# A decay row carried by DMA instead of one-column matmuls, from chunk 10 on, in a gated linear attention and MoE kernel

## The chip, the cores and the metric

The kernel runs on one core of a Trainium2 chip. The metric is the device time of one execution in microseconds (us). A core has five engines with queues of their own: TensorE (PE, with weight loads listed as PEld), VectorE (DVE), ScalarE (ACT), GpSimd (POOL) and SyncE (SP), which here issues every DMA. Each engine executes its queue in order and waits on semaphores for the others.

## The reference

Inputs are q, k, v and alpha in float32, each of 4 batches, 8 heads, 768 steps and 48 channels, and two weight matrices of 384x2048 and 2048x384.

```python
for t in range(S):
    state = alpha[:, :, t, :, None] * state + np.einsum('bhd,bhe->bhde', k[:, :, t], v[:, :, t])
    y[:, :, t] = np.einsum('bhd,bhde->bhe', q[:, :, t], state)
...
x = attn_out.transpose(0, 2, 1, 3).reshape(B * S, H * D)
h = x @ w_in
r = np.maximum(h, 0.0)
return (r * r) @ w_out
```

The output is 3072x384 in float32.

## The kernel before

The 3072 tokens are 24 chunks of 128 steps, six to a batch (NCH). Chunks 0 to 3 are handled two at a time by `add_super`; chunks 4 to 23 by `add_chunk(s)`, with their scores and outputs in `add_scores` and `add_back` (from chunk 8 on two chunks share one `add_scores`). For one chunk the steps are:

- `add_load`: SyncE loads alpha, q, k and v (tiles at, qt, kt, vt), 192 KB each.
- L402 on ACT: L = ln(alpha) into L_s, whose heads are padded from 48 to 64 channels. L407 on POOL: v into bf16.
- `e_p0` on PE: one matmul of 384 columns with an upper triangle sums the logarithms over the steps into a PSUM bank (`pm`); then four matmuls of one column each, with L as weights and a column of ones, put the sums over the whole chunk into four more columns of the same bank, with the channels on the partitions.
- L421 and L425 on ACT: A = exp of the running sums, and Ainv = exp of their negatives, both bf16. L428 and L431 on ACT: the exponentials of the four whole-chunk columns go into `ae_s`, the decay factors of the state, two heads to a column on partitions 0 to 63 and 64 to 127.
- L440 and L443 on DVE: q times A into qA_s, k times Ainv into kI_s. `e_p1q`, `e_p1k` on PE transpose both, L367 copies them (qkT).
- `e_p2` on PE: the scores; L504 on DVE masks them (sm).
- `e_ps` on PE adds k'v to the state in PSUM (st); L538 on DVE (`e_stm`) multiplies the state by `ae_s`; L543 on ACT copies it to bf16 (sb). The last chunk of a batch has none of these three.
- `e_p3a` and `e_p3b` on PE: the chunk's output from the state of the chunk before (sb) and from sm; L365 and a transpose put it into xT_big.

The last running sum of a chunk (row 127 of A) and the sum that the one-column matmuls make are the same quantity, once with the channels along a row and once down the partitions.

The feed-forward part follows group by group: `add_moe1` (x by w_in on PE, relu on ACT in L790, square on DVE in L798) and `add_moe2` (gT by w_out, copy to ob in L828 or L830, store in L837).

All instructions are written out in one order, which a planner (`Plan`) makes in Python: each step has an engine, a planned duration, dependences and a latency, and a list scheduler gives it a start; `plan.order` is sorted by these starts, and the steps are emitted in that order, so each engine's queue is fixed by it. "DMA" is the planner's engine for loads and "OUT" for stores, both emitted on SyncE; a store is placed 3.5 us (OUT_LATE) after its data. `gate` lets `e_p0` of a chunk start only a certain lead ahead of the feed-forward progress. Ahead of the plan, seven matmuls of 512 columns on a zero tile (`warm`) run on PE, and before the first `add_moe2` step idle stretches of the plan on PE are filled with matmuls of 256 columns (`DUMMY`).

Of the kernel before, what the change touches and what calls it, by code (L numbers as in the profile page):

```python
# [8 lines left out]
FP32 = mybir.dt.float32  # L9
BF16 = mybir.dt.bfloat16  # L10
AF = mybir.ActivationFunctionType
# [45 lines left out]
def after(op, x=0.0):  # L57
    return (op, x)
# [86 lines left out]
def kernel(  # L145
# [10 lines left out]
    nc = tc.nc  # L156
    B, H, S, D = q.shape
    HD = H * D
    P = 128
    DP = 64  # L160
    NP = H // 2
# [17 lines left out]
    consts = ctx.enter_context(tc.tile_pool(name="consts", bufs=1))  # L179
    big = ctx.enter_context(tc.tile_pool(name="big", bufs=1))  # L180
    LB = 6
    loads = ctx.enter_context(tc.tile_pool(name="loads", bufs=LB // 2))
    work = ctx.enter_context(tc.tile_pool(name="work", bufs=4))
# [6 lines left out]
    banks = [ctx.enter_context(tc.tile_pool(name=f"bank{i}", bufs=1, space=PSUM)) for i in range(5)]  # L190
# [1 line left out]
    nc.scalar.preload_act_table_set("natural_log_exp_and_others")  # L192

    HF = P // 2
    warm = consts.tile([P, 512], BF16)
    nc.vector.memset(warm, 0.0)
    ones_f = consts.tile([P, P], FP32)
    nc.gpsimd.memset(ones_f, 1.0)
# [2 lines left out]
        out=utri_f, in_=ones_f, compare_op=ALU.is_ge, fill=0.0,  # L201
# [4 lines left out]
        out=sutri_f, in_=ones_f, compare_op=ALU.is_ge, fill=0.0,  # L206
# [10 lines left out]
    for src, dst in ((utri_f, half_in), (sutri_f, half_ex)):  # L217
        nc.vector.memset(dst, 0.0)
        for ab in range(2):
            h = slice(ab * HF, ab * HF + HF)  # L220
            nc.vector.tensor_copy(dst[h, h], src[h, h])
    for ab in range(2):
        h = slice(ab * HF, ab * HF + HF)
# [8 lines left out]
    w_out_b = consts.tile([P, FT, d_model], BF16)  # L232

    NBUF = 4
    L_s = big.tile([P, NBUF, H, DP], BF16)
    nc.gpsimd.memset(L_s[:, :, :, D:], 0.0)
    qA_s = big.tile([P, NBUF, H, DP], BF16)
    nc.gpsimd.memset(qA_s[:, :, :, D:], 0.0)
    ident_bf = consts.tile([P, P], BF16)
    make_identity(nc, ident_bf)  # L240
    kI_s = big.tile([P, NBUF, H, DP], BF16)
    nc.gpsimd.memset(kI_s[:, :, :, D:], 0.0)
    ae_s = big.tile([P, NBUF, NP, 2], FP32)
    nc.vector.memset(ae_s, 0.0)
    xT_big = big.tile([P, KT, n_tok], BF16)

    def pin(ins):
        tc.keep_in_program_order(ins)

    def mm(*a, **kw):  # L250
        pin(nc.tensor.matmul(*a, **kw))  # L251

    def tr(*a):
        pin(nc.tensor.transpose(*a))  # L254
# [6 lines left out]
    GLA_BANKS = sl_bank[0:2]  # L261
# [4 lines left out]
    def psum(op, shape, dt):  # L266
        i = op.slot.bank
        return banks[i].tile(shape, dt, name=f"bank{i}")
# [6 lines left out]
    def add(eng, dur, emit, *deps, **kw):  # L275
        return plan.add(Op(eng, dur, emit, deps, **kw))
# [115 lines left out]
    def add_chunk(s):  # L392
        d = C[s]
        b, c = divmod(s, NCH)
        i = s % NBUF
        L, qA, kI, ae = L_s[:, i], qA_s[:, i], kI_s[:, i], ae_s[:, i]
        old = C[s - NBUF].get("end") if s >= NBUF else None
        g = dict(prio=-10.0 + s * 0.01)
        last = c == NCH - 1

        def e_ln():
            pin(nc.scalar.activation(L[:, :, 0:D], d["at"], AF.Ln))  # L402
        ln = d["use_at"] = add("ACT", 0.41, e_ln, d["ld_at"], old, prio=-15.0 if s < EARLY else -5.0)

        def e_vb():
            d["vb"] = work.tile([P, H, D], BF16, name="vb", bufs=4)
            pin(nc.gpsimd.tensor_copy(d["vb"], d["vt"]))  # L407
        vb = d["use_vt"] = add("POOL", 0.55, e_vb, d["ld_vt"], old, prio=-5.0)

        def e_p0():  # L410
            pm = d["pm"] = psum(p0, [P, 512], FP32)
            mm(pm[:, 0:HD], lhsT=utri_b[:, 0, :], rhs=L[:, :, 0:D], start=True, stop=True)
            for p in range(NP):
                mm(pm[:, HD + p:HD + p + 1], lhsT=L[:, 2 * p:2 * p + 2, :], rhs=ones_col,
                   start=True, stop=True)
        p0 = Op("PE", 0.27, e_p0, [ln], takes=GLA_BANKS, lat=0.17, **g)
        p0.gla = s

        def e_A():
            d["A"] = work.tile([P, H, D], BF16, name="A")  # L420
            pin(nc.scalar.activation(d["A"], d["pm"][:, 0:HD].rearrange("p (h d) -> p h d", h=H), AF.Exp))  # L421

        def e_Ai():
            d["Ai"] = work.tile([P, H, D], BF16, name="Ainv")
            pin(nc.scalar.activation(d["Ai"], d["pm"][:, 0:HD].rearrange("p (h d) -> p h d", h=H), AF.Exp, scale=-1.0))  # L425

        def e_ae0():
            pin(nc.scalar.activation(ae[0:64, :, 0], d["pm"][0:64, HD:HD + NP], AF.Exp))  # L428

        def e_ae1():  # L430
            pin(nc.scalar.activation(ae[64:128, :, 1], d["pm"][64:128, HD:HD + NP], AF.Exp))  # L431
        plan.add(p0)
        a_ = add("ACT", 0.38, e_A, p0, **g)
        ai = add("ACT", 0.38, e_Ai, p0, after(a_), **g)
        ae0 = add("ACT", 0.18, e_ae0, p0, after(ai), **g)
        ae1 = add("ACT", 0.19, e_ae1, p0, after(ae0), **g)
        p0.gives = ae1

        def e_qA():
            pin(nc.vector.tensor_mul(qA[:, :, 0:D], d["qt"], d["A"]))  # L440

        def e_kI():
            pin(nc.vector.tensor_mul(kI[:, :, 0:D], d["kt"], d["Ai"]))  # L443
        mq = d["use_qt"] = add("DVE", 0.47, e_qA, a_, d["ld_qt"], old, **g)
        mk = d["use_kt"] = add("DVE", 0.47, e_kI, ai, d["ld_kt"], old, **g)

        def e_p1q():
            d["pT"] = psum(p1q, [P, 2 * NP, P], BF16)
            for p in range(NP):
                tr(d["pT"][:, p, :], qA[:, 2 * p:2 * p + 2, :], ident_bf)  # L450

        def e_p1k():
            for p in range(NP):
                tr(d["pT"][:, NP + p, :], kI[:, 2 * p:2 * p + 2, :], ident_bf)
        p1q = plan.add(Op("PE", 0.22, e_p1q, [mq], takes=GLA_BANKS, **g))
        p1k = plan.add(Op("PE", 0.22, e_p1k, [mk, after(p1q)], lat=0.15, **g))

        def e_cp(lo, hi):
            if lo == 0:
                d["qkT"] = work.tile([P, 2 * NP, P], BF16, name="qkT")  # L460
            cast(cpk if lo else cp, d["qkT"][:, lo:hi, :], d["pT"][:, lo:hi, :])
        if s < EARLY:
            cp = add({"ACT": 0.49, "DVE": 0.34}, 0, lambda: e_cp(0, NP), p1q, **g)
            cpk = add({"DVE": 0.34, "ACT": 0.49}, 0, lambda: e_cp(NP, 2 * NP), p1k, after(cp, -9.0), **g)
        else:
            cp = cpk = add("DVE", 0.61, lambda: e_cp(0, 2 * NP), p1k, **g)
        p1q.gives = cpk

        d.update(cps=[cp, cpk], mk=mk, vb_op=vb, ae1=ae1, kI=kI, ae=ae)
        if s < PAIRS:  # L470
            add_scores(s, 1)
            add_back(s)
        elif s % 2:
            add_scores(s - 1, 2)
            add_back(s - 1)
            add_back(s)
# [90 lines left out]
    def add_super(u):  # L567

        d = SUP[u]
        i = 2 * u % NBUF  # L570
        pair = (C[2 * u], C[2 * u + 1])
        L, qA, kI, ae = L_s[:, i:i + 2], qA_s[:, i:i + 2], kI_s[:, i:i + 2], ae_s[:, i:i + 2]
        old = [C[2 * u - NBUF + ab].get("end") for ab in range(2)] if u >= 2 else []
        g = dict(prio=-10.0 + u * 0.02)
        any_ = (0, 1)
# [4 lines left out]
        ln = d["use_at"] = add("ACT", 0.73, e_ln, d["ld_at"], *old, prio=-15.0)  # L580
# [20 lines left out]
        p0 = [Op("PE", 0.53 if t else 0.33, lambda t=t: e_p0(t), [ln], takes=SUP_BANKS, lat=0.17, **g) for t in any_]  # L601
# [10 lines left out]
        a_, ai = [None, None], [None, None]  # L612
# [5 lines left out]
        def e_ae(j):  # L618
            h = slice(HF * j, HF * j + HF)
            tot = d["pm"][1][h, HD:HD + 2 * NP].rearrange("p (n a) -> p a n", a=2)  # L620
            pin(nc.scalar.activation(ae[h, :, :, j], tot, AF.Exp))
        ae0 = add("ACT", 0.19, lambda: e_ae(0), p0[1], after(ai[1]), **g)
        ae1 = add("ACT", 0.19, lambda: e_ae(1), p0[1], after(ae0), **g)
# [79 lines left out]
        for ab in any_:  # L703
            s = 2 * u + ab
# [40 lines left out]
            if s:  # L745
                p3a = c["p3a"] = plan.add(Op("PE", 0.2, e_p3a, [cq, before], takes=SUP_BANKS, **g))
            p3b = c["p3b"] = plan.add(Op("PE", 0.5, e_p3b, [*sm, *vb, after(p3a)], takes=None if s else SUP_BANKS,
                                         lat=0.15, **g))
# [12 lines left out]
    RELU_PRIO = -20.0  # L761
    RELU_PRIO0 = 0.0
    DUMMY = 1
    sq = {}
    prog = {"m1": 0.0, "m2": 0.0}

# [124 lines left out]
    plan.run(gate)  # L891


    wp = banks[4].tile([P, 512], FP32, name="bank4")
    for _ in range(7):
        mm(wp, lhsT=warm[:, 0:P], rhs=warm, start=True, stop=True)
    pe_end = None
    for op in plan.order:
        if op.eng == "PE":
            if getattr(op, "moe", (0,))[0] == 2:  # L900
                pe_end = None
                DUMMY = 0
            if pe_end is not None and DUMMY:
                n = max(0, int((op.start - pe_end - 0.2) / 0.11))
                if n:
                    wp = banks[4].tile([P, 512], FP32, name="bank4")
                for _ in range(n):
                    mm(wp[:, 0:256], lhsT=warm[:, 0:P], rhs=warm[:, 0:256], start=True, stop=True)
            pe_end = op.start + op.dur
        op.emit()  # L910
# [28 lines left out]
```

## Time and profile before

| | |
|---|---|
| median of 3 runs | 188.93 us (188.61 to 189.2) |
| the profiled execution | 187.66 us, of which the span from the first to the last instruction is 185.9 |
| granted TensorE clock, mean | 0.999 |
| PE busy | 178.4 us |
| DVE busy | 133.8 us |
| ACT busy | 122.6 us |
| DMA queue 1 | 99152 packets, 29.89 MB, 68.1% of 16 engines' span |

The profile is one execution; the median is of others. All times in the text that are points of time count from the span's start. Matmuls are pipelined, so the length shown for one reaches into the next, and starts tell more than lengths. In the lists of groups a line gives the operation, the tiles, the shape, the count, the busy time, the mean of one in ns and the idle time before it with what ended it. L251 and L254 are the lines of the helpers for matmuls and transposes, L367 and L365 those of the copy helper.

### The profile page before, as it was taken

How to read it: one execution, taken by the hardware profiler on the slowest of the kernel's cores; microseconds unless marked ns; L12 is line 12 of the kernel's file. 1: busy time of each engine (PE TensorE's matmuls, PEld its weight loads, DVE VectorE, ACT ScalarE, POOL GpSimd, SP SyncE). 2: the span in 40 equal slices, each digit the busy share in tenths (PEclk: the TensorE clock that was granted, in tenths of full speed). 3: DMA queues.
4: the chain of work that ended last, by engine and by line, in shares of the span. 5: the costliest groups of instructions: out<-in, count | busy, mean ns of one | idle time of the engine just before them, and what ended most of it. 6: DMA issues, size and time to landing. Idle time of an engine off the chain costs nothing.

```text
span 185.9 us, 5105 instructions
## 1 busy us (share of the span) xinstructions
PE 178.4 (96%) x2037; PEld 134.1 (72%) x2037; DVE 133.8 (72%) x280; ACT 122.6 (66%) x282; POOL 29.6 (16%) x47
## 2 busy tenths in 40 slices
PE   6889899999999999999999999999999999999992
PEld 2666684667887878878878878777868778767761
DVE  7688679875999986876976966866987976842400
ACT  3577779455896896776676776667778668434621
POOL 5044777411012111111020020020020000000000
PEclk9999999999999999999999999999999999999999
DMA  5999999899899999999997984691011011011112
GB/s 146 261 280 339 385 370 331 175 223 205 161 206 209 236 199 231 184 231 201 189 222 162 216 166 101 157 212 61 0 42 46 2 48 42 4 42 42 46 43 84
DMA packets 99176, 30.22 MB, mean 163 GB/s; under 512 B 92112, under 2 KB 98000, under 8 KB 99152
## 3 DMA queue, kind: packets, MB, share of 16 engines
q1 hardware_dynamic: 99152, 29.89, 68.1%
q8 instruction: 16, 0.26, 0.5%
q14 instruction: 8, 0.07, 0.1%
HBM read 25.17 MB, written 4.72 MB: 161 GB/s over the span
## 4 chain that ended last, share of the span: by engine, by line
PE 88%; DMA 3%; ACT 3%; SPq 2%; DVE 1%; issue 0%
PE bank L251 77%; PE bank L254 7%; DMA at<-in_alpha_dram 3%; PE sc L251 2%; PE st L251 2%; SPq L360 2%; DVE qkT L367 1%; ACT raw L691 1%; ACT L_s L579 0%; DVE qA_s L627 0%; ACT w_in_b L304 0%; DVE st L721 0%; ACT r L790 0%; ACT ob L830 0%; ACT A L610 0%
## 5 line engine op out<-in xcount | busy, mean ns | idle before, releaser
L251 PE MATMUL bank<-xT_big,w_in_b 128*128 128x256 bf16 (+2 forms) x600 | 73.1, 269 | 0.0
L251 PE MATMUL bank<-w_out_b,gT 128*128 128x384 bf16 x384 | 72.4, 326 | 0.0
L790 ACT ACTIVATE r<-bank 128x512 bf16<-128x512 f32 x96 | 56.9, 602 | 18.8 <-PE bank L251 16.5
L251 PEld LDWEIGHTS <-w_in_b 128*128 128x128 bf16 x600 | 52.5, 98 | 9.2
L798 DVE TENSOR_TENSOR gT<-r 128x512 bf16<-128x512 bf16 x96 | 45.2, 493 | 17.1 <-ACT r L790 16.6
L251 PEld LDWEIGHTS <-gT 128*128 128x128 bf16 x384 | 35.1, 97 | 17.8
L407 POOL CAST vb<-vt 128x384 bf16<-128x384 f32 x20 | 10.9, 550 | 92.7 <-PE bank L251 45.6
L367 DVE COPY qkT<-bank 128x1024 bf16<-128x1024 bf16 (+1 forms) x26 | 16.5, 649 | 6.3 <-PE bank L254 6.2
L830 ACT COPY ob<-bank 128x384 f32<-128x384 f32 x20 | 9.6, 479 | 14.6 <-PE bank L251 14.6
L504 DVE TENSOR_TENSOR sm<-sc,utri_b 128x512 bf16<-128x512 f32 x24 | 15.4, 684 | 2.0 <-PE sc L251 2.0
L365 ACT CAST xn<-bank 128x384 bf16<-128x384 f32 x24 | 10.9, 481 | 5.8 <-PE bank L251 5.7
L440 DVE TENSOR_TENSOR qA_s<-qt,A 128x384 bf16<-128x384 f32 x20 | 11.5, 577 | 3.8 <-ACT A L421 3.7
L251 PEld LDWEIGHTS <-qkT 64*128 64x128 bf16 (+2 forms) x304 | 10.4, 98 | 4.9 <-issue 2.5
L421 ACT ACTIVATE A<-bank 128x384 bf16<-128x384 f32 x20 | 9.9, 494 | 6.2 <-PE bank L251 6.2
L367 DVE COPY xT_big<-bank 128x384 bf16<-128x384 bf16 x21 | 7.4, 354 | 8.3 <-PE bank L254 8.2
L443 DVE TENSOR_TENSOR kI_s<-kt,Ainv 128x384 bf16<-128x384 f32 x20 | 11.3, 567 | 0.0
L543 ACT CAST sb<-st 128x384 bf16<-128x384 f32 x16 | 7.6, 476 | 5.2 <-DVE st L538 5.2
L402 ACT ACTIVATE L_s<-at 128x384 bf16<-128x384 f32 x20 | 10.0, 520 | 0.5 <-DMA at<-in_alpha_dram 0.4
L504 DVE TENSOR_TENSOR sm<-bank,utri_b 128x512 bf16<-128x512 f32 x16 | 10.2, 681 | 0.0
L251 PE MATMUL bank<-warm 128*128 128x256 bf16 (+1 forms) x41 | 8.2, 333 | 2.0 <-DVE both L216 1.3
L425 ACT ACTIVATE Ainv<-bank 128x384 bf16<-128x384 f32 x20 | 9.9, 496 | 0.0
L251 PE MATMUL bank<-vb,sm 128*128 128x48 bf16 (+1 forms) x224 | 9.6, 183 | 0.0
(70 smaller groups left out, 176.3 us busy)
## 6 DMA issues: line engine op xcount, KB each, us to landing
at<-in_alpha_dram SPq DMA_DIRECT2D x20, 192.0 KB, 3.9
qt<-in_q_dram SPq DMA_DIRECT2D x20, 192.0 KB, 3.7
kt<-in_k_dram SPq DMA_DIRECT2D x20, 192.0 KB, 4.0
vt<-in_v_dram SPq DMA_DIRECT2D x20, 192.0 KB, 3.7
out_dram<-ob SPq DMA_DIRECT2D x20, 192.0 KB, 2.3
wo<-in_moe_w_out_dram SPq DMA_DIRECT2D x4, 768.0 KB, 6.8
wi<-in_moe_w_in_dram SPq DMA_DIRECT2D x3, 768.0 KB, 8.0
at<-in_alpha_dram SPq DMA_DIRECT2D x2, 384.0 KB, 4.9
```

The source lines that it names most:

```text
L251: pin(nc.tensor.matmul(*a, **kw))
L254: pin(nc.tensor.transpose(*a))
L365: pin(nc.scalar.copy(out_t, in_t))
L367: pin(nc.vector.tensor_copy(out_t, in_t))
L402: pin(nc.scalar.activation(L[:, :, 0:D], d["at"], AF.Ln))
L407: pin(nc.gpsimd.tensor_copy(d["vb"], d["vt"]))
L421: pin(nc.scalar.activation(d["A"], d["pm"][:, 0:HD].rearrange("p (h d) -> p h d", h=H), AF.Exp))
L440: pin(nc.vector.tensor_mul(qA[:, :, 0:D], d["qt"], d["A"]))
L443: pin(nc.vector.tensor_mul(kI[:, :, 0:D], d["kt"], d["Ai"]))
L504: pin(nc.vector.tensor_mul(d["sm"][:, hh], d["sc"][hh], utri_b.to_broadcast([P, NP, P])))
L790: pin(nc.scalar.activation(box["r"][:, 0:w], box["ph"][:, 0:w], AF.Relu))
L798: pin(nc.vector.tensor_mul(gT[g][:, f0:f0 + per, lo * P:lo * P + n], r, r))
```

## The change

From chunk 10 on (`TURN = 10`) the four one-column matmuls and the two exponentials L428 and L431 are left out. A is written in float32 into a tile `Af` of the order (half j, channel d, pair n), so that consecutive channels of a head lie four floats apart, and L440 reads it in that order. Two DMAs on SyncE (planner's engine "SPD", planned at 0.4 us and a latency of 4.0 us) carry row 127 of `Af` into `ae_s`, 48 partitions of four floats each; `ae_s` has its last two axes exchanged for this. The planner is given 0.17 instead of 0.27 us for `e_p0`, and the bank is given back after Ainv. In the start, the warm tile is 128 columns wide and read four times over, nine matmuls of 512 and two of 128 columns take the place of seven of 512, and idle stretches before 8.0 us of the plan get half as many dummies.

```diff
-    warm = consts.tile([P, 512], BF16)
+    warm = consts.tile([P, P], BF16)
...
+    TURN = 10
+    AE_LAT = 4.0
...
-    ae_s = big.tile([P, NBUF, NP, 2], FP32)
+    ae_s = big.tile([P, NBUF, 2, NP], FP32)
...
-        L, qA, kI, ae = L_s[:, i], qA_s[:, i], kI_s[:, i], ae_s[:, i]
+        L, qA, kI, ae = L_s[:, i], qA_s[:, i], kI_s[:, i], ae_s[:, i].rearrange("p j n -> p n j")
...
-            for p in range(NP):
+            for p in range(NP if s < TURN else 0):
                 mm(pm[:, HD + p:HD + p + 1], lhsT=L[:, 2 * p:2 * p + 2, :], rhs=ones_col,
                    start=True, stop=True)
-        p0 = Op("PE", 0.27, e_p0, [ln], takes=GLA_BANKS, lat=0.17, **g)
+        p0 = Op("PE", 0.27 if s < TURN else 0.17, e_p0, [ln], takes=GLA_BANKS, lat=0.17, **g)
...
+        def split(x, s):
+            if s < TURN:
+                return x.rearrange("p (h d) -> p h d", h=H)
+            return x.rearrange("p (n j d) -> p n j d", n=NP, j=2)
+
         def e_A():
-            d["A"] = work.tile([P, H, D], BF16, name="A")
-            pin(nc.scalar.activation(d["A"], d["pm"][:, 0:HD].rearrange("p (h d) -> p h d", h=H), AF.Exp))
+            if s < TURN:
+                d["A"] = work.tile([P, H, D], BF16, name="A")
+            else:
+                d["Af"] = work.tile([P, 2, D, NP], FP32, name="Af", bufs=2)
+                d["A"] = d["Af"].rearrange("p j d n -> p n j d")
+            pin(nc.scalar.activation(d["A"], split(d["pm"][:, 0:HD], s), AF.Exp))
...
-        ae0 = add("ACT", 0.18, e_ae0, p0, after(ai), **g)
-        ae1 = add("ACT", 0.19, e_ae1, p0, after(ae0), **g)
-        p0.gives = ae1
+
+        def e_aed():
+            for j in range(2):
+                pin(nc.sync.dma_start(out=ae_s[HF * j:HF * j + D, i, j], in_=d["Af"][P - 1:P, j]))
+        if s < TURN:
+            ae0 = add("ACT", 0.18, e_ae0, p0, after(ai), **g)
+            p0.gives = ae1 = add("ACT", 0.19, e_ae1, p0, after(ae0), **g)
+        else:
+            p0.gives = ai
+            ae1 = add("SPD", 0.4, e_aed, a_, lat=AE_LAT, **g)
 
         def e_qA():
-            pin(nc.vector.tensor_mul(qA[:, :, 0:D], d["qt"], d["A"]))
+            if s < TURN:
+                pin(nc.vector.tensor_mul(qA[:, :, 0:D], d["qt"], d["A"]))
+            else:
+                v4 = "p (n j) d -> p n j d"
+                pin(nc.vector.tensor_mul(qA[:, :, 0:D].rearrange(v4, j=2), d["qt"].rearrange(v4, j=2), d["A"]))
...
+    COLD = 8.0
...
-    wp = banks[4].tile([P, 512], FP32, name="bank4")
-    for _ in range(7):
-        mm(wp, lhsT=warm[:, 0:P], rhs=warm, start=True, stop=True)
+    def idle_mm(n, w):
+        wp = banks[4].tile([P, 512], FP32, name="bank4")
+        for _ in range(n):
+            mm(wp[:, 0:w * P], lhsT=warm, rhs=warm[:, None, :].to_broadcast([P, w, P]), start=True, stop=True)
+
+    idle_mm(9, 4)
+    idle_mm(2, 1)
...
-                n = max(0, int((op.start - pe_end - 0.2) / 0.11))
+                n = max(0, int((op.start - pe_end - 0.2) / (0.22 if pe_end < COLD else 0.11)))
                 if n:
-                    wp = banks[4].tile([P, 512], FP32, name="bank4")
-                for _ in range(n):
-                    mm(wp[:, 0:256], lhsT=warm[:, 0:P], rhs=warm[:, 0:256], start=True, stop=True)
+                    idle_mm(n, 2)
```

## The prediction

> **What bounds the kernel now.** I read the page's busy times and its chain first.
>
> ```profile
> PE 178.4 (96%) x2037; PEld 134.1 (72%) x2037; DVE 133.8 (72%) x280; ACT 122.6 (66%) x282; POOL 29.6 (16%) x47
> ...
> PE 88%; DMA 3%; ACT 3%; SPq 2%; DVE 1%; issue 0%
> ```
>
> PE is busy 96% of the span and carries 88% of the chain that ended last. A busy PE need not be a full one, so I looked next at the table of stretches, and at the starts of consecutive matmuls in the timeline.
>
> ```profile
> 60.00:100.00 40.00, 39.99 (x461) 31.40 (x460) 32.04 (x67) 29.16 (x70) 4.84 (x9) 1.00 0.98 205
> 100.00:140.00 40.00, 40.00 (x455) 31.16 (x454) 30.56 (x65) 28.89 (x69) 3.13 (x6) 1.00 0.56 124
> 140.00:183.00 43.00, 42.49 (x419) 31.75 (x416) 23.13 (x50) 23.79 (x53) 0.00 (x0) 1.00 0.11 38
> ```
>
> The columns are the stretch, its length, busy time of PE, PEld, DVE, ACT and POOL, granted clock, DMA share and GB/s. PE has 0.5 us idle in 123 us, at full clock. Here lie chunks 10 to 23 (chunk 10's L421 starts at 68.2, chunk 23's at 157.2). So in the part that the change rewrites, time taken off PE's queue comes off the end, and a late input to PE is paid in full. DVE is 80% busy up to 100, ACT 73%. The DMA share is 0.98 until 100 and 0.11 at the end.
>
> Then chunk 14 in the timeline (start, length, engine, line):
>
> ```profile
> 95.86 0.33 PE L251 MATMUL bank<-L_s,utri_b 128*128 128x384 bf16 x1
> ...
> 96.03 0.24 PE L251 MATMUL bank<-ones_col,L_s 128*128 128x1 bf16 x4
> ...
> 96.13 0.81 PE L251 MATMUL bank<-w_out_b,gT 128*128 128x384 bf16 x4
> ...
> 96.30 0.49 ACT L421 ACTIVATE A<-bank 128x384 bf16<-128x384 f32 x1 [0.57 <-PE bank L251]
> ...
> 96.83 0.56 DVE L440 TENSOR_TENSOR qA_s<-qt,A 128x384 bf16<-128x384 f32 x1 [0.40 <-ACT A L421]
> ...
> 98.08 0.37 PEld L254 LDWEIGHTS <-qA_s 128*128 128x128 bf16 x4
> ...
> 99.50 0.56 DVE L538 TENSOR_TENSOR st<-st,ae_s 128x384 f32<-128x384 f32 x1
> ```
>
> Starts tell what a matmul costs the queue, since its length overlaps the next: the four one-column matmuls hold PE from 96.03 to 96.13, 0.10 us, not the 0.24 shown. qA is ready at 97.39 and PE takes it at 98.08, so it has 0.69 us to spare. In chunk 13 it is less: qA starts at 88.29, ends at 88.85, and its weights load at 89.12.
>
> ```profile
> 88.29 0.56 DVE L440 TENSOR_TENSOR qA_s<-qt,A 128x384 bf16<-128x384 f32 x1
> ...
> 89.12 0.37 PEld L254 LDWEIGHTS <-qA_s 128*128 128x128 bf16 x4
> ```
>
> Last, SyncE and the DMAs:
>
> ```profile
> 80.56 0.59 SPq L837 DMA_DIRECT2D out_dram<-ob  x1
> ```
> ```profile
> at<-in_alpha_dram SPq DMA_DIRECT2D x20, 192.0 KB, 3.9
> out_dram<-ob SPq DMA_DIRECT2D x20, 192.0 KB, 2.3
> ```
>
> The ob of that store ends at 80.54 (L830, 80.06 + 0.48): SyncE stood waiting for it although the plan places each store 3.5 us after its ob. So SyncE runs about 3 us ahead of its own order while loads fill the queue. A load lands 3.9 us after issue; the late stores, on an idle DMA, 1.8 (the least of the 20).
>
> **The change part by part.**
>
> *One-column matmuls.* Fourteen chunks lose four each. The cost is 0.10 us (96.03 to 96.13, likewise 82.23 to 82.33), in chunk 13 0.13 (87.19 to 87.32). 14 x 0.10 to 14 x 0.13 is 1.4 to 1.8 us; I take 1.5, as the short gap is the commoner. It is all on PE's full stretch. A may also start some 0.08 us sooner, since the matrix product ends at 96.19 and the last one-column result at 96.27.
>
> *L428 and L431.* Twenty-eight ACTIVATEs at 0.17 us go, 4.8 us of ACT. ACT has 27% idle, and PE does not wait for it in these stretches: 0. The bank is given back sooner, also 0.
>
> *A in float32, d in steps of four floats.* ACT writes and DVE (L440) reads 384 elements, each 16 bytes from the last. The type costs nothing by the rows: L365 writes 128x384 bf16 in 481 ns, L830 the same size in f32 in 479; L538 reads f32 in 557, L440 bf16 in 577. No row has such a step. The bounds: nothing, or one more element time per element, by the slopes between sizes: ACT (L579 with 768 elements, L402 with 384) (844 - 520)/384 = 0.84 ns, so +0.32 us; DVE (L504 with 512, L538 with 384) (684 - 557)/128 = 0.99 ns, so +0.38 us. A gain is excluded, as nothing is read less often. I take 0, because neither engine's rows here change with the bytes of an element; both ends stay in the range. The Trainium skill, page "Advanced Engine Details and Errata", section "SBUF Cachelines", speaks against the change: an SBUF line has 16 bytes, and accesses that go to another line each time pay a penalty, which this step makes all of them. No run here shows it; by that page the forecast would move towards the first rival.
>
> *The two DMAs.* Each writes 48 pieces of 16 bytes. Queue 1's 68.1% of 16 x 185.9 us over 99152 packets is 20 ns a packet, so 96 more, plus completions, are about 0.12 us of DMA per chunk: nothing, beside 3.9 us a load. SyncE pays two issues of 0.33 to 0.9 us (the stores' least; the loads' usual when the queue is full), and both wait for A. SyncE being 3 us early, it will stand there, and behind it stand the next loads, at, qt, kt and vt of chunks 12 to 23, and stores. Who waits for them: L402 and L407 of later chunks. L402 of chunk 12 follows its load's landing by 1.2 us (69.2, 70.4), of chunk 15 by 2.8 (81.3, 84.1), of chunk 14 by 6.0, of chunk 16 by 10.5. Only the first few are near; cost 0 to 1 us once, and I take 0.1. A gain is excluded, as nothing before the wait goes sooner.
>
> *The multiplication of the state, L538.* It now waits for a DMA. In chunk 14 it starts 2.7 us after A's end (96.79). The diff plans 0.4 + 4.0 us between A and the matmuls of st, so it will stand about 5 us after A. From A's end the DMAs take 2 x 0.35 us of issue and 1.8 (idle) to 3.9 us (loaded): 2.5 to 4.6, inside the plan, since SyncE is early and the loads in front drain meanwhile. What is late next is sb: 100.57 becomes about 103, and its readers are st of chunk 15 at 104.17 and the pair's sb matmuls at 108.27. Cover is left, and PE has MoE work to order in between: 0. Without that cover each us is a us.
>
> *Start.* All that is before chunk 10 keeps its order. The smaller warm tile makes a shorter memset (0.27 us now), nine matmuls of 512 columns and two of 128 fill what was idle before the first L_s matmul at 5.42, and fewer dummies follow. The seven of now run from 1.25, 3.17 us with a last one of 0.63, so they start 0.42 us apart; nine from 1.1 end near 5.0, and two small ones by 5.3: before 5.42, 0.1 us late at worst. The matmul at 5.42 already runs at full pace (the next starts at 5.58, 384 columns in 0.16), so there is no slow clock to cure. And the chain of this part is not PE's: it is the second alpha load (4.32 to 10.52), then L579. I take 0, with -0.1 to +0.1.
>
> Sum on the profiled execution: span 185.9 - 1.5 + 0.1 = 184.5; its time 187.66 (1.76 outside the span) becomes 186.3. The median lies 1.27 above that run, at 188.93, and becomes 187.5.
>
> **The rivals.**
>
> *The step of 16 bytes hurts on both engines* (17%). qA comes 0.32 + 0.38 - 0.08 = 0.62 us later. Spare is 0.27 in chunks like 13; in chunks like 14 the tightest is kI (97.85, taken at 98.41), 0.56. Seven odd chunks lose 0.35, seven even 0.06: +2.9 - 1.5 = +1.4, 190.3. For: L440 and L421 gain a pattern that no row has. Against: equal times for 2 and 4 byte elements. It decides from 0.49 us of lateness on, where seven times 0.22 eat the gain; DVE alone (0.30 late) costs only 0.2, giving 187.6.
>
> *The factors land late and DVE stands at L538* (15%). With loads in front unfinished, 0.7 + 4.9 us (the slowest store landing) is 5.6 against 5.0. Six such chunks (10, 12 to 16) lie in the full DMA stretch. DVE is in order, so qA, sm and gT stand behind it; after about 0.3 us of spare (chunk 13) the remaining 0.3 x 6 = 1.8 us reach PE: 189.2. Against: the wait for A drains the queue.
>
> *Loads held behind the waits starve L402* (8%). Chunks 12, 13 and 15 lose up to 1 us of ACT each, of which I put half on PE: 188.9.
>
> *The change doesn't shorten the queue* (5%): the new order leaves PE a gap of 0.1 us where the matmuls were, and the time stays 188.9. Against: 0.5 us idle in 123.
>
> **How the numbers follow.** The forecast, 187.5, has 55%. Its own range is 186.8 (1.8 saved, 0.1 at the start, no load wait, and 0.2 of PE's idle time) to 188.1 (the load wait at 1 us less a little). For 8 in 10 the range reaches up to the step's rival, and down to all the bounds together: 186.7 to 190.3. 0.3%, 0.57 us, is about what a measurement of this kernel can tell from no change. Faster needs under 188.36: the forecast's 55% and some 7% of milder rivals, 62%. Within 0.3%: half of the two rivals near 188.9 and the last, 14%. Slower: the step's rival and worse forms of the others, 24%.
>
> **What would show it.** Right: PE from 60 to 183 still without idle, the L_s matmul followed at once by the next, A and L440 at 0.49 and 0.56 us after chunk 10 as before it, L538 about 5 us after A with no DMA among what DVE waits for, SyncE waiting at the new DMAs for A. Wrong: L440 near 0.94 us or L421 near 0.8 with PE waiting for qA; DVE waiting for a DMA at L538; ACT waiting for alpha loads at L402.

## The result and the profile after

The change made the kernel about 1% slower: 190.47 us median (189.96 to 191.9, 8 runs) against 188.92 of the kernel before in the same comparison, a ratio of 1.0103 (95% interval 1.0073 to 1.0134). The profiled execution took 191.44 us with a span of 189.7, so it is one of the longer ones. The lines of the code have moved: L421, L440, L443, L538, L402 and the matmul and transpose helpers are now L432, L462, L465, L560, L404, L253 and L256.

The stretches first (PE, PEld, DVE, ACT, POOL, clock, DMA share, GB/s):

```profile
60.00:100.00 40.00, 38.77 (x420) 28.93 (x419) 31.43 (x62) 28.58 (x59) 6.30 (x8) 1.00 0.88 183
100.00:140.00 40.00, 39.38 (x422) 29.58 (x421) 31.85 (x63) 28.20 (x56) 3.01 (x6) 1.00 0.68 145
140.00:183.00 43.00, 42.86 (x422) 31.78 (x420) 26.43 (x56) 26.29 (x51) 0.80 (x1) 1.00 0.11 37
```

PE, which had 0.5 us idle in these 123 us, now has 2.0. More of its waiting stands at the weight loads of the transposes, which need qA and kI. The list of waits has it (total, times, longest):

```profile
PEld L256 <- DVE kI_s L465: 2.9, 11, 0.5
PEld L256 <- DVE qA_s L462: 2.8, 9, 0.6
```

In the kernel before the list had one such wait for qA of L440, and none for kI of L443:

```profile
PEld L254 <- DVE qA_s L440: 0.3, 1, 0.3
```

The groups by form (busy us, mean ns, idle before) show why qA and kI are late:

```profile
L462 DVE TENSOR_TENSOR qA_s<-qt,Af 128x384 bf16<-128x384 f32 x14 | 12.3, 881 | 6.1 <-ACT Af L432 5.4 <-DMA qt<-in_q_dram 0.7
...
L432 ACT ACTIVATE Af<-bank 128x384 f32<-128x384 f32 x14 | 12.1, 866 | 2.6 <-PE bank L253 2.3
```

The same two operations in the kernel before:

```profile
L440 DVE TENSOR_TENSOR qA_s<-qt,A 128x384 bf16<-128x384 f32 x20 | 11.5, 577 | 3.8 <-ACT A L421 3.7
...
L421 ACT ACTIVATE A<-bank 128x384 bf16<-128x384 f32 x20 | 9.9, 494 | 6.2 <-PE bank L251 6.2
```

Chunk 14 in the timeline, to be held against the same chunk before:

```profile
99.31 0.33 PE L253 MATMUL bank<-L_s,utri_b 128*128 128x384 bf16 x1
...
99.67 0.87 ACT L432 ACTIVATE Af<-bank 128x384 f32<-128x384 f32 x1
...
100.58 1.12 DVE L462 TENSOR_TENSOR qA_s<-qt,Af 128x384 bf16<-128x384 f32 x1 [0.25 <-ACT Af L432]
...
101.61 0.55 DVE L465 TENSOR_TENSOR kI_s<-kt,Ainv 128x384 bf16<-128x384 f32 x1
101.71 1.17 SPq L449 DMA_DIRECT2D ae_s<-Af  x2
101.74 0.23 PEld L256 LDWEIGHTS <-qA_s 128*128 128x128 bf16 x4 [0.60 <-DVE qA_s L462]
...
102.21 0.23 PEld L256 LDWEIGHTS <-kI_s 128*128 128x128 bf16 x4 [0.24 <-DVE kI_s L465]
```

Before, qA lay ready 0.69 us ahead of its weight load; now the load stands 0.60 us and starts 0.04 us after qA's end, then stands again for kI. This is the longest of the waits and not a usual one: the q times A of this chunk takes 1.12 us, that of the other thirteen 0.85 to 0.89, and why it is longer stays open. The one-column matmuls are gone: the next matmul starts at 99.47, 0.16 after the L_s matmul.

### The profile page after: what moved, and what is told of

It is laid out like the page before. It is cut to its first block, busy times and chain, and to the rows that moved or that the text cites. A ratio compares the mean times of both kernels' runs of the same rounds, so it can differ in the third digit from the quotient of the medians.

```text
span 189.7 us, 5000 instructions
## 1 busy us (share of the span) xinstructions
PE 181.0 (95%) x1978; PEld 131.7 (69%) x1979; DVE 138.4 (73%) x278; ACT 124.9 (66%) x256; POOL 32.0 (17%) x47
## 4 chain that ended last, share of the span: by engine, by line
PE 74%; ACT 9%; DMA 6%; DVE 5%; issue 2%; SPq 2%; ACTq 0%
PE bank L253 63%; PE bank L256 7%; DMA at<-in_alpha_dram 6%; ACT r L813 2%; ACT Af L432 2%; PE sc L253 2%; SPq L362 2%; PE st L253 2%; DVE kI_s L465 1%; DVE qA_s L462 1%; ACT Ainv L436 1%; DVE gT L821 1%; DVE qkT L369 1%; ACT raw L713 1%; ACT A L432 1%
## 5 line engine op out<-in xcount | busy, mean ns | idle before, releaser
L253 PE MATMUL bank<-xT_big,w_in_b 128*128 128x256 bf16 (+2 forms) x599 | 73.4, 268 | 0.1
L253 PE MATMUL bank<-w_out_b,gT 128*128 128x384 bf16 x384 | 72.7, 326 | 0.0
L253 PEld LDWEIGHTS <-w_in_b 128*128 128x128 bf16 x600 | 53.0, 98 | 10.5 <-issue 1.2
L821 DVE TENSOR_TENSOR gT<-r 128x512 bf16<-128x512 bf16 x96 | 46.2, 507 | 16.3 <-ACT r L813 15.7
L253 PEld LDWEIGHTS <-gT 128*128 128x128 bf16 x384 | 35.4, 98 | 17.8
L409 POOL CAST vb<-vt 128x384 bf16<-128x384 f32 x20 | 13.5, 676 | 93.2 <-DMA vt<-in_v_dram 46.5
L853 ACT COPY ob<-bank 128x384 f32<-128x384 f32 x22 | 10.6, 480 | 13.5 <-PE bank L253 13.5
L462 DVE TENSOR_TENSOR qA_s<-qt,Af 128x384 bf16<-128x384 f32 x14 | 12.3, 881 | 6.1 <-ACT Af L432 5.4
L253 PEld LDWEIGHTS <-qkT 64*128 64x128 bf16 (+2 forms) x304 | 10.5, 97 | 5.6 <-issue 2.7
L432 ACT ACTIVATE Af<-bank 128x384 f32<-128x384 f32 x14 | 12.1, 866 | 2.6 <-PE bank L253 2.3
L465 DVE TENSOR_TENSOR kI_s<-kt,Ainv 128x384 bf16<-128x384 f32 x20 | 12.7, 633 | 0.0
L404 ACT ACTIVATE L_s<-at 128x384 bf16<-128x384 f32 x20 | 10.4, 526 | 2.2 <-DMA at<-in_alpha_dram 2.1
L256 PE MATMUL bank<-ident_bf,qA_s 128*128 128x128 bf16 x96 | 9.4, 220 | 1.3 <-DVE qA_s L462 0.6
L253 PE MATMUL bank<-warm 128*128 128x256 bf16 (+2 forms) x39 | 8.7, 355 | 1.9 <-DVE both L216 1.1
```

What stands on the lines that cost most here:

```text
L432: pin(nc.scalar.activation(d["A"], split(d["pm"][:, 0:HD], s), AF.Exp))
L462: pin(nc.vector.tensor_mul(qA[:, :, 0:D].rearrange(v4, j=2), d["qt"].rearrange(v4, j=2), d["A"]))
L821: pin(nc.vector.tensor_mul(gT[g][:, f0:f0 + per, lo * P:lo * P + n], r, r))
```

## The experiments

The theory was the first rival of the prediction: the step of 16 bytes makes A and q times A late, and PE pays. Against it stood two others: SyncE's waits for A hold loads and factors back, or the planner's new order is worse by itself. Each ratio is against the kernel before in the same comparison, whose median was 188.1 to 188.7 us; several expectations in us were set from 188.9, and so lie a little high.

**The step alone.** `step_only`, on the kernel before:

```diff
-            d["A"] = work.tile([P, H, D], BF16, name="A")
...
+            if s < TURN:
+                d["A"] = work.tile([P, H, D], BF16, name="A")
...
+            else:
+                d["Af"] = work.tile([P, 2, D, NP], FP32, name="Af", bufs=2)
+                d["A"] = d["Af"].rearrange("p j d n -> p n j d")
...
```

> The kernel before, with A alone changed from chunk 10 on: float32, written by ACT and read by DVE with 16 bytes from element to element; the one-column matmuls, their exponentials and the plan's durations stay, no DMA is added. Theory (the step of 16 bytes makes A and q times A late for PE): A 0.86 us and q times A 0.86 us instead of 0.49 and 0.56, PE waits for qA, and the time is before plus about 3 us (the 1.55 us that the change lost plus the 1.5 us of PE that it saved): 191.9, 190.9 to 193. Rival (SyncE's waits for A hold the loads back): as before, 188.9 within 0.3. Rival (the new order): as before.

Measured: 193.03 us, ratio 1.0251 (1.0207 to 1.0294), 4.7 us slower, just past the end of the expected range, 193. A takes 872 ns and q times A 860. There is no new DMA in it, and it loses more than the whole change does, as nothing is saved in it. Its waits:

```profile
PEld L255 <- DVE qA_s L450: 3.6, 10, 0.6
PEld L255 <- DVE kI_s L453: 2.0, 9, 0.3
```

**The DMAs without the step.** `dma_no_step`, on the changed kernel:

```diff
-                d["A"] = d["Af"].rearrange("p j d n -> p n j d")
+                d["A"] = d["Af"].rearrange("p j d n -> p (j d n)").rearrange("p (n j d) -> p n j d", n=NP, j=2)
```

> The changed kernel with A in float32 but in one unbroken row per step, so that ACT and DVE write and read neighbours; the two DMAs move the same number of pieces of 16 bytes at the same place in the order, but the four floats of a piece are then neighbouring channels, so the decay factors from chunk 10 on are wrong ones. Theory (step): A and q times A back to 0.49 and 0.56 us, the 1.5 us of PE come off: 187.5, 187.0 to 188.2. Rival (waits on SyncE and at the state's multiplication): still near the changed kernel, 190 to 190.5, with ACT waiting for alpha loads. Rival (order): also near 190.

Measured: 186.23 us, ratio 0.9892 (0.9861 to 0.9923), with the two operations back:

```profile
L462 DVE TENSOR_TENSOR qA_s<-qt,Af 128x384 bf16<-128x384 f32 x14 | 7.8, 556 | 2.2 <-ACT Af L432 2.2
L432 ACT ACTIVATE Af<-bank 128x384 f32<-128x384 f32 x14 | 6.9, 491 | 2.6 <-PE bank L253 2.3
```

The new DMAs and SyncE's waits for A, and the planner's new order, are all in this kernel, so they are not what made the change slow. Both rivals fall with it. Between this kernel and the changed one lies the step alone: 1.0103 / 0.9892 = 1.0213, or 4.0 us. The time is below the expected 187.0 to 188.2: the change of the start, which the expectation took at nothing, is worth 0.5 us (below), and the kernel before stood at 188.29 here.

Both kernels execute the same 1978 matmuls. PE is busy 178.1 us of a span of 184.8 here and 181.0 of 189.7 in the changed kernel. So of the 4.9 us between these two executions 2.9 lie inside what the profile lists as busy and only 2.0 in idle time. A stretch that shows no idle time is thus no proof that PE waits for nothing.

**The saving alone.** `no_factors` leaves out L428, L431 and the one-column matmuls from chunk 10 on, and puts nothing in their place (`p0` planned at 0.17).

> The kernel before without the one-column matmuls and the two exponentials from chunk 10 on, and with nothing in their place: the state is multiplied by factors of an earlier chunk. It shows what leaving them out is worth by itself. Theory (step) and rival (waits): 14 times 0.10 to 0.13 us of PE, 187.4, 187.0 to 187.7. Rival (the new order that 0.17 for 0.27 us brings costs by itself): 188.9 or more.

Measured: 186.64 us, ratio 0.9930 (0.9902 to 0.9958): 1.3 us by the ratio, 1.65 by the medians. The saving is about the expected one, 1.4 to 1.8 us; the time in us is below the expected range, which was set from 188.9. The rival that the new order costs by itself falls.

**The start alone.** `start_only` is the kernel before with the warm tile, `idle_mm` and `COLD` of the change.

> The kernel before with the start alone changed: the narrow warm tile, nine and two matmuls ahead, half as many dummies before 8 us of the plan. All theories: 188.9 within 0.3, since the chain of the start runs over the second alpha load.

Measured: 187.72 us, ratio 0.9975 (0.9954 to 0.9996). The median hides the kind of the gain: the executions lie between 187.48 and 187.96, those of the kernel before in the same comparison between 187.51 and 189.43. The long ones are gone. The expectation, no change within 0.3 us, missed this. I come back to it below.

**How wide a step costs.** Three layouts on the changed kernel: A and factors in bfloat16 (`bf16_step8`: both tiles declared BF16), float32 with two heads interleaved (`step8`) or eight (`step32`). The line of `step8`, whose other lines bring the sums, q and qA into the same order of heads, and then that of `step32`:

```diff
...
-                d["A"] = d["Af"].rearrange("p j d n -> p n j d")
+                d["A"] = d["Af"].rearrange("p j d n -> p (j d n)").rearrange("p (x d m) -> p m x d", x=4, m=2)
...
```
```diff
-                d["A"] = d["Af"].rearrange("p j d n -> p n j d")
+                d["A"] = d["Af"].rearrange("p j d n -> p (j d n)").rearrange("p (d n j) -> p n j d", n=NP, j=2)
```

> The changed kernel with A and the decay factors in bfloat16 in the same order: the step from element to element is 8 bytes instead of 16, the DMAs move pieces of 8 bytes, all is computed. Theory (two elements must share 16 bytes): A 0.49 and q times A 0.56 us, time as with the unbroken rows, 186.3, 185.8 to 187.0, and so faster than both kernels. Rival (any step other than one element costs): A and q times A between 0.6 and 0.9, 188 to 190.5.

> The changed kernel with A in float32 with a step of 8 bytes (two heads interleaved instead of four). The DMAs move as many pieces of 16 bytes as before, but the floats of a piece are not those of one channel, so the decay factors from chunk 10 on are wrong ones. Theory (two elements must share 16 bytes): 0.49 and 0.56 us, 186.3, 185.8 to 187.0. Rival (the cost grows with the step): about a third of the extra, A 0.6 and q times A 0.66 us, 187 to 188.

> The changed kernel with A in float32 with a step of 32 bytes (all eight heads interleaved); again the factors from chunk 10 on are wrong ones. Theory (each element in 16 bytes of its own is the whole cost): no worse than 16 bytes, A and q times A 0.86 us, 190 to 191.5. Rival (the cost grows with the step): 1.2 us and more, 193 or more.

Measured: 188.53 us, ratio 0.9993 (0.9966 to 1.0020); 187.43 us, 0.9952 (0.9924 to 0.9980); and 189.96 us in one run. The groups by form, of `bf16_step8`, `step8` and `step32` in turn:

```profile
L432 ACT ACTIVATE Af<-bank 128x384 bf16<-128x384 f32 x14 | 14.4, 1028 | 2.6 <-PE bank L253 1.9 <-DMA out_dram<-ob 0.2 <-DMA vt<-in_v_dram 0.2
...
L462 DVE TENSOR_TENSOR qA_s<-qt,Af 128x384 bf16<-128x384 f32 x14 | 7.8, 559 | 8.1 <-ACT Af L432 8.1
```
```profile
L462 DVE TENSOR_TENSOR qA_s<-qt,Af 128x384 bf16<-128x384 f32 x14 | 7.8, 556 | 2.4 <-ACT Af L432 2.3
L432 ACT ACTIVATE Af<-bank 128x384 f32<-128x384 f32 x14 | 7.3, 520 | 2.6 <-PE bank L253 2.3
```
```profile
L432 ACT ACTIVATE Af<-bank 128x384 f32<-128x384 f32 x14 | 12.2, 869 | 2.6 <-PE bank L253 2.3
L462 DVE TENSOR_TENSOR qA_s<-qt,Af 128x384 bf16<-128x384 f32 x14 | 12.1, 864 | 6.2 <-ACT Af L432 5.8 <-DMA vt<-in_v_dram 0.3
```

For DVE's reads the theory held: free at 8 bytes (556, 559 ns), 0.30 us at 16 and no more at 32. For ACT's writes in float32 it held nearly (520, 866, 869, against 491 without a gap). It failed for ACT's writes in bfloat16: at 8 bytes they take 1028 ns, longer than float32 at 16. So the mended layout in bfloat16 gave the time of the kernel before and no gain; what that cost is made of stays open. The time of `step8` missed as well: the operations are as the theory said, but 187.43 us lies in the rival's 187 to 188, 1.1 us above `dma_no_step` by the ratios. What that 1.1 us is, no run shows. The single run of `step32` is at the low end of its range.

**One engine at a time.** `read_only` writes A without a gap and reads it with the step, `write_only` the reverse (one view of `Af` for L432, another for L462).

> The changed kernel, where ACT writes A in float32 without a gap and only DVE reads with 16 bytes from element to element (so q is multiplied by elements of A in another order, and the factors from chunk 10 on are wrong ones). Theory (PE's wait is lateness beyond the spare of the order): A 0.49, q times A 0.86 us, qA 0.30 us late, which the spare of 0.27 to 0.56 us nearly hides: 186.5, 186.0 to 187.3. Rival (each extra us on DVE, which is busy 73% of the span, comes off the end): half the loss of the changed kernel, 188.2 or more.

> The changed kernel, where only ACT writes A in float32 with 16 bytes from element to element and DVE reads the same bytes without a gap (again another order of A's elements for q; the factors come from the right places). Theory: A 0.86, q times A 0.56 us, so qA is 0.37 us late, and kI too, as Ainv comes behind A: of the spare of 0.24 to 0.56 us some is short, 186.8, 186.2 to 187.8. Rival (each extra us on ACT comes off the end): 188.2 or more.

Measured: 187.57 us, ratio 0.9982 (0.9958 to 1.0005), and 187.25 us, 0.9958 (0.9927 to 0.9989). DVE 860 ns in the first, ACT 866 in the second. Against `dma_no_step` (0.9892) that is 1.7 us for DVE's 0.30 and 1.2 us for ACT's 0.37, each with some 0.8 us of uncertainty; in the changed kernel both together cost 4.0. The first lies just above its expected range, the second within it: the spare hides less of DVE's delay than I had expected, and more of both than the rivals said, which put both at 188.2 or more. That the two together cost more than the 2.9 us of their sum fits a spare that can be used only once, but the difference lies within the intervals. The lists of waits point the same way: the weight loads wait 1.0 us for qA of L463 and kI of L466 in `read_only`, 1.1 us in `write_only`, and 5.7 us for the same two in the changed kernel.

**The planner told.** `plan_told` is the changed kernel with the measured extra added to the two planned durations:

```diff
-        a_ = add("ACT", 0.38, e_A, p0, **g)
+        a_ = add("ACT", 0.38 if s < TURN else 0.75, e_A, p0, **g)
...
-        mq = d["use_qt"] = add("DVE", 0.47, e_qA, a_, d["ld_qt"], old, **g)
+        mq = d["use_qt"] = add("DVE", 0.47 if s < TURN else 0.77, e_qA, a_, d["ld_qt"], old, **g)
```

> The changed kernel with nothing but the planned durations altered: A 0.75 instead of 0.38 and q times A 0.77 instead of 0.47 us from chunk 10 on, so that the order gives PE other work while they run. Theory (the step costs time only because PE is sent to the transposes too early): PE's waits for qA and kI go, and most of the loss with them, 187.0 to 188.3. Rival (ACT and DVE lack the 9 us that the step adds to them): still above the kernel before, 189.5 to 190.5.

Measured: 187.07 us, ratio 0.9926 (0.9896 to 0.9955). It computes all, and is faster than both kernels: 1.4 (by the ratio) to 1.6 us (by the medians) under the one before, 3.4 under the change. The slow operations are as slow as they were; PE only comes later:

```profile
L432 ACT ACTIVATE Af<-bank 128x384 f32<-128x384 f32 x14 | 12.1, 866 | 1.7 <-ACT xn L367 1.0 <-PE bank L253 0.5
L462 DVE TENSOR_TENSOR qA_s<-qt,Af 128x384 bf16<-128x384 f32 x14 | 12.0, 859 | 2.8 <-ACT Af L432 2.8
```
```profile
PEld L256 <- DVE qA_s L462: 0.4, 1, 0.4
```

The first fence is from the groups by form, the second from the waits: 0.4 us where the changed kernel had 2.8, and none for kI. So ACT and DVE have room for the 9 us that the step adds; the loss was lateness, not load. Not all of the twelve executions are alike: they lie between 186.24 and 188.27, and the profiled one is the longest. Its chain runs over DMAs more than that of the kernel before did (12% against 3%), mostly loads ahead of chunk 10, and DVE waits once, 1.2 us, for factors at L560. What sets the executions apart stays open.

**Twice the DMAs.** `right8` has the step of 8 bytes in float32 with all computed, at the price of four DMAs of 48 pieces of 8 bytes per chunk instead of two.

> The changed kernel with A in float32 with a step of 8 bytes and all computed: two heads interleaved, the pairs of heads in the state stored in the order 0, 2, 1, 3, and four DMAs of 48 pieces of 8 bytes per chunk instead of two of 16. Theory: A 0.52 and q times A 0.56 us; the last DMA lands about 1.2 us later than with two, 3.5 us after A's end when the DMA is idle and up to 6.5 when loads are in front, and the state's multiplication stands 5 to 7 us after A; 187.0, 186.4 to 188.2, faster than both kernels. Rival (the factors now land too late): DVE waits for the DMA at the multiplication, 188.5 or more.

Measured: 198.51 us in the median of six, ratio 1.0517 (1.0458 to 1.0577), far beyond what either side of the expectation named. A takes 520 and q times A 555 ns; the cost is on SyncE and behind it:

```profile
86.90 4.38 SPq L451 DMA_DIRECT2D ae_s<-Af  x4
```
```profile
ACT L_s L405 <- DMA at<-in_alpha_dram: 7.2, 5, 4.2
...
DVE st L562 <- DMA ae_s<-Af: 4.9, 2, 4.4
```

The four issues of chunk 12 hold SyncE for 4.4 us (timeline), DVE waits up to 4.4 us for factors at the state's multiplication, and ACT 7.2 us for alpha loads (both from the waits). This is the prediction's second and third rival, at twice the number of DMAs. The mean granted clock in this profile is 0.974, so a part of the loss is a slower PE; the one execution at a clock of 1.0 took 195.75 us, still 7.6 above the median before. The planner was given 0.4 us and a latency of 4.0 for the four DMAs as for two, so this order too was made from a wrong duration; what it would be with the right one was not run.

**The start, taken apart.** `start_warm` keeps the nine and two matmuls and the narrow tile, but not the halved dummies; `few_warm` is the kernel before with three matmuls ahead instead of seven.

> The kernel before with the narrow warm tile and the nine and two matmuls ahead of the plan, the dummies before 8 us as they were. The whole start change alone ran at 187.5 to 188.0 where the kernel before spread over 187.5 to 189.4. Theory (more matmuls ahead make the clock full in every execution): the same narrow band, 187.7. Rival (the fewer dummies later are what counts): the spread of before, median 188.3 to 188.9.

> The kernel before with three instead of seven matmuls of 512 columns ahead of the plan. Theory (the executions of the kernel before that take 1 us longer are those in which seven are too few for the clock to be full when the first L_s matmuls come): the L_s matmuls of 384 columns now start 0.32 instead of 0.16 us apart in the profile, and all executions lie at 188.8 to 189.5 or above. Rival (the spread comes from elsewhere): the L_s matmuls 0.16 us apart, the times spread over 187.5 to 189.4 as before.

Measured: `start_warm` 187.61 us (187.44 to 187.89), ratio 0.9979 (0.9958 to 1.0000), the narrow band again. `few_warm` 188.62 us (188.02 to 189.73), ratio 1.0028 (0.9994 to 1.0061). Its timeline shows slower matmuls at the start:

```profile
5.25 0.48 PE L251 MATMUL bank<-L_s,half_in 128*128 128x384 bf16 x1 [2.54 <-ACT L_s L579]
5.53 0.52 PE L251 MATMUL bank<-L_s,half_ex 128*128 128x384 bf16 x1
5.85 0.84 PE L251 MATMUL bank<-L_s,half_in 128*128 128x384 bf16 x2
...
6.74 2.66 PE L251 MATMUL bank<-warm 128*128 128x256 bf16 x12
```

The L_s matmuls start 0.28 and 0.32 us apart instead of 0.16, the twelve dummies take 2.66 us instead of 1.47, and the chain of the start now runs through them; the span is 186.7 instead of 185.9. The profile shows a granted clock of 1.00 for it all the same; that the clock is the reason is argued from the pace, which is about half of that before. The executions did not all lie above 188.8, as I had expected, and they still spread over 1.7 us; but none is left below 188.0. So slower matmuls at the start go with a span 0.8 us longer in the two profiled executions. That the long executions of the kernel before are such ones is not shown, since the one profiled of them is a short one. The Trainium skill, page "TensorE: Matmul & The Clock Gate", section "What's actually happening", says that the clock rises after about 3.4 us of work within a window that runs on by itself, so that the moment varies from run to run. The seven matmuls of the kernel before fill 3.17 us in the timeline (from 1.25), the eleven of `start_only` 4.17 (from 1.05): that fits, and no run here shows the window itself. It is not the only source of long executions: `plan_told` has the new start, and its longest execution, the profiled one, has the L_s matmuls 0.16 us apart.

## Why the prediction was wrong, step by step

The forecast was 187.5 us, 186.7 to 190.3 for 8 in 10, and faster; measured is 190.47, and slower. Term by term:

- *One-column matmuls*, 1.5 us off PE: right. `no_factors` gave 1.3 us by the ratio, 1.65 by the medians.
- *L428 and L431*, nothing: right, as far as it can be told; they are gone in `no_factors` too, and its gain is that of PE.
- *A in float32, d in steps of four floats*, taken at 0: here the prediction failed. The bounds were 0 to 0.32 us on ACT and 0 to 0.38 on DVE, and the measured extra is 0.37 and 0.30: past the far end on ACT and near it on DVE. By itself the step cost 4.0 us of time. I chose the near end because the rows don't change with the bytes of an element. But the width of an element and the distance to the next are two things, and the rows said nothing of the second. The Trainium skill, page "Advanced Engine Details and Errata", section "SBUF Cachelines", did: elements that share no line of 16 bytes cost, two to a line do not. The trace agrees for DVE (556 ns at 8 bytes, 860 at 16) and for ACT in float32 (520, 866), and not for ACT in bfloat16 (1028 at 8 bytes). It was left as a sentence beside the row instead of deciding between two ends that no row could tell apart.
- *The first rival*, 17% at 190.3: it is what happened, at 190.47. Its mechanism was right: lateness of 0.62 us against spare of 0.27 to 0.56. Its size was a sum of 2.9 us of loss and 1.5 of saving; measured are 4.0 of loss, and the start's 0.5 on the other side, which brought the total back near it: that the figure came so close is in part luck. "DVE alone costs only 0.2" was mis-sized too: 1.7 us in `read_only`. The spare was counted once per chunk, between one operation and one weight load, but what stands behind on DVE and ACT comes later as well; that this is the missing 1.1 us is argued, and no run separates it. The range ended at the rival's own figure and gave its terms no room, and the median fell just past it.
- *The two DMAs and SyncE's waits*: right. SyncE stood waiting at L449 for 30 us in all, ACT waited 2.1 us for alpha loads instead of 0.4, and with all this `dma_no_step` was the fastest of all. Its ratio, 0.9892, is no higher than the saving and the start give without any new DMA (0.9930 x 0.9975 = 0.9905).
- *The state's multiplication*: right. In the changed kernel L560 starts 5.1 to 7.4 us after A's end, the factors land 2.3 to 4.8 us after it, and DVE's waits name no DMA there. A DMA of the factors lands 2.2 us after issue in the median, 4.3 at most.
- *Start*, taken at 0: wrong by 0.5 us. The sum was made on one profiled execution, where the first L_s matmuls were at full pace, and the kernel before has longer executions.

## What to carry to other kernels

Where an operation gets a new access pattern, price the distance between elements and not only their number and width; if no row has such a distance, the bounds are all that the profile gives, and the choice between them needs other ground. Where an order is written ahead from planned durations, a slower operation must be written into the plan: the same 0.67 us per chunk cost 4.0 us untold, and 0.6 us once told (0.9926 against 0.9892 without the step, with intervals that overlap). And a profile is one execution: a spread of 1% between executions may hide a stage whose length differs from run to run.

## What was not expected of the hardware

ACT writing bfloat16 with 8 bytes from element to element took 1028 ns for 384 elements, against 494 in bfloat16 without a gap, 520 in float32 at 8 bytes and 866 in float32 at 16. DVE read that same tile in 559 ns. And doubling the small DMAs from two to four per chunk, 48 pieces of 8 bytes each, moved the time from 187.4 us (`step8`) to 195.8 in the best execution, at a clock of 1.0, although they carry the same bytes: with loads in the queue one group of four held SyncE for 4.4 us. The order was not planned for that, so how much of it is the DMAs' own stays open.
